# A gated state-space block with its backward pass on one core: half-array products side by side, kernel sums in one run, wide parameter products, single weight transposes, stores from GpSimd

## The chip, the cores and the metric

The kernel runs on one core of a Trainium2 chip. The core has a matrix engine (PE, with its weight loads listed as PEld), a vector engine (DVE), a scalar engine (ACT), a general engine (POOL, also called GpSimd), a sync engine (SP) that here only issues DMAs, and 16 DMA engines. SBUF is the on-chip memory, PSUM the memory that matrix products are added up in[...]. The metric is the device time of one execution in microseconds (us); the median of several runs is compared.

## What is computed

The reference is a block of one sequence of L = 2048 tokens and D = 576 channels, and its gradients for a given output gradient. Everything is bf16 in memory.

```python
xn = layernorm(x)                                   # x: 2048 x 576
K[d,l] = Re sum_n C[d,n] * exp(dt[d]*A[d,n]*l) * dt[d]*B[d,n]      # n = 128 states
s  = causal_convolution(xn, K) + xn * Dskip         # reference: by FFT along the tokens
h  = silu(xn @ w1) * (xn @ w3)                      # w1, w3: 576 x 4608
g  = silu(h @ w2)                                   # w2: 4608 x 576
out = x + s * g
# returned: out and the gradients of x, A, B, C (real and imaginary), log_dt, Dskip, w1, w3, w2
```

## The kernel before

All of it is one program of some 42,000 instructions, written with tile pools: a tile is a buffer of a pool, and a new tile of the same name waits until an earlier one of that name is free. The instructions of each engine run in one fixed order. That order is made when the program is built, by a list scheduler: `at(us)` (line 83) gives what follows a due time, and instructions that could go next are taken by due time. The due times are a planner's numbers and not times of the chip; changing one moves instructions in an engine's order.

The work, by its place in the trace of before:

- **0 to 133 us, prologue.** Layer norm, the transposed activations xnT, selectors and exponentials for the convolution kernel, spectra of the input.
- **133 to 531, forward products and kernel sums.** `ffn_hidden` (L688) makes the gate and up products: for each of 9 blocks of 512 hidden columns and each of 16 token tiles, one PSUM tile `pgu` of two banks. D = 576 is four full slices of 128 rows and a rest of 64. The full slices are L719. The two rests, of w1 and of w3, lie in the lower and the upper half of the partitions of one weight tile `wtail`, and their products (L720, L721) use half of the array's rows each. ACT and DVE evict `pgu` (L722, L724, L725); SP stores h and POOL stores gate and up (`gu_t` to `GI_dram`, L728). Between them `ssm_kernel` (L418) makes the convolution kernel in 36 chunks of 16 channels: `kgen_chunk` (L455) makes the factors q (stored to `Q_dram`), pz (three planes: minus P, Z, P; POOL makes the first as the negative of the third at L477; stored to `PZ_dram`), and v; `kgen_sum` (L490) multiplies q by v in 64 small products into `kps` (L500), each of 64 output rows by 16 columns. Each channel of a sum has its own due time, spread over the chunk's share.
- **531 to 830, forward tail.** `forward_tail` (L731): h by w2 (nine weight tiles `w2g`, loaded by POOL at L769), silu, the spectral convolution, and the transposes of the gradient `go_o` into `goT` (L833, four of 128 columns and one of 64 for each tile of tokens).
- **about 800 to 1593, hidden gradients.** `backward` (L1079) takes 18 groups of 256 hidden columns. `phase6_load` loads gate and up into tiles of the ring X and Y (L1193, L1194, POOL) and w2 rows (`w2r`, POOL, L1152) which SP transposes into `w2T`; `phase6_group` (L1211) multiplies `goT` by `w2T` into `ph` (L1226), ACT casts it to `gh` (L1229), DVE multiplies it into the two hidden gradients (L1232), and the weight gradients follow (L1273 and the functions `phase6_grad2`, `phase6_grad13`). The hidden gradients are stored by SP to `GU_dram` and `GG_dram` at the group's end (L1239). Until about 1300 `conv_bwd_quarter` (L886) makes the backward convolution beside this, with sums over the partitions by a column of ones (L917), and stores its spectra to `gK_dram`.
- **from 1300, parameter chunks.** `param_chunk` (L970), 36 of them, 19 beside the last groups and 17 beside the input gradient. Each loads the spectra gz, a transposed q (`qT`) and pz, makes two half chunks of products in two PSUM tiles `et_ps` each (L989), multiplies them by the planes of pz with DVE (L996, two sums s times two parts r) and reduces them into `S_all` (L998). Five `final_block`s (L1010) turn `S_all` into the gradients of A, B, C and dt; their due times stand in `final_at`.
- **1593 to 2000, input gradient.** `phase6_inputs` (L1288): for 16 tiles of tokens the two hidden gradients are read transposed (`ggc`, `guc`) and multiplied by the transposed w1 and w3 (L1333). These weights are made by DMA transposes from DRAM in `wT_into` (L1131), one for each of the five slices of D, into `wTA` (12 of 36 blocks, early), `wTB` (12), the memory of goT (4) and of go_o (8).

All DMA transposes are issued by SP through `nat_transpose` (L1140).

## Time and profile before

| | us |
|---|---|
| median of five runs | 2008.13 |
| the five runs | 2001.21, 2006.64, 2008.13, 2019.79, 2030.61 |
| the profiled execution | 2002.15 |
| its span, first to last instruction | 2000.4 |
| busy: PE, DVE, ACT, POOL | 1764.7, 1419.9, 1024.6, 269.5 |
| PE: gate and up products (L719) | 283.8 |
| PE: the two 64-row tails (L720, L721), in the stretch 133 to 531 | 55.9 each, side by side |
| PE: kernel sums (L500), in the same stretch | 57.1 |
| DVE: parameter products (L996) and reduces (L998) | 186.7 and 175.7 |
| POOL: negation of a factor (L477) | 55.5 |

The mean granted clock of PE in this execution was 0.965 of full speed. A row of instruction groups names line, engine, operation, output and inputs, shapes and count, then the busy time in us and the mean duration in ns of one, then the idle time of the engine just before them and what ended it. A row of a timeline begins with start and duration in us, and ends, in brackets, with the idle time before it and its releaser. An engine name with q (SPq) means that the row is the issuing of a DMA. Matmuls are pipelined: a duration of 0.39 us can stand for a start every 0.216.

### The profile page before, as it was taken

The page shows a single profiled execution, that of the slowest core. Times are in us where ns is not written, and L with a number is a line of the kernel's source. Part 1 is how long each engine was busy: PE and PEld are TensorE (multiplying, and loading weights), DVE is VectorE, ACT ScalarE, POOL GpSimd, SP SyncE. Part 2 cuts the span into 40 slices and gives each one's busy share as a digit, 9 for nine tenths or more (in the row PEclk, how much of TensorE's full clock was granted, in tenths as well). Part 3 has the DMA queues.
Part 4 walks back from the last instruction along what each step waited for, and adds up shares of the span by engine and source line. Part 5 has one row for each costly group of instructions (what it writes and reads, how often), then busy time and mean ns, then how long its engine had stood idle before and what let it go on. Part 6 is the DMA issues. An engine that isn't in the chain of part 4 may idle for free. (4 is left out here: it accounts for less than half of the span.)

```text
span 2000.4 us, 41956 instructions
## 1 busy us (share of the span) xinstructions
PE 1764.7 (88%) x17179; PEld 1292.0 (65%) x17179; DVE 1419.9 (71%) x2660; ACT 1024.6 (51%) x1739; POOL 269.5 (13%) x362
## 2 busy tenths in 40 slices
PE   2789999999889988989889898969999967989788
PEld 1544444444478866877778777758787845767666
DVE  7538888888477753486983859748989913489686
ACT  2778888888545555765666646526445200100112
POOL 4003333333322221000000000100000000000000
PEclk9899999999899999999999999989999978999999
DMA  3579888787966687365563654798998999999992
GB/s 86 190 284 320 308 292 297 275 313 277 301 188 157 164 216 230 114 185 165 172 185 112 184 160 151 191 246 226 237 233 219 208 197 187 198 197 218 211 187 58
DMA packets 612906, 417.10 MB, mean 209 GB/s; under 512 B 400394, under 2 KB 558058, under 8 KB 607978
## 3 DMA queue, kind: packets, MB, share of 16 engines
q1 hardware_dynamic: 547200, 280.47, 56.6%
q0 software_dynamic: 24288, 106.94, 15.5%
q10 hardware_dynamic: 41226, 27.02, 5.0%
q8 instruction: 134, 2.20, 0.5%
q14 instruction: 58, 0.48, 0.1%
HBM read 134.06 MB, written 188.01 MB: 161 GB/s over the span
## 5 line engine op out<-in xcount | busy, mean ns | idle before, releaser
L719 PE MATMUL pgu<-wmB_w,xnT 128*128 128x512 bf16 x1152 | 283.8, 382 | 1.2 <-ACT E_k L392 1.2
L1273 PEld LDWEIGHTS <-xn_bf 128*128 128x128 bf16 x2304 | 223.9, 98 | 29.3 <-issue 2.5
L1273 PE MATMUL pgw<-Y,xn_bf 128*128 128x256 bf16 x2048 | 232.1, 273 | 1.7 <-ACT gw L1275 1.6
L996 DVE TENSOR_TENSOR pr_q<-et_ps,pz 128x512 f32<-128x512 f32 x288 | 186.7, 686 | 42.5 <-PE et_ps L989 37.2
L1226 PE MATMUL ph<-w2T,goT 128*128 128x256 bf16 x1440 | 190.1, 280 | 22.8 <-ACT gh L1229 22.7
L719 PEld LDWEIGHTS <-xnT 128*128 128x128 bf16 x1152 | 103.5, 98 | 124.9 <-issue 20.4
L998 DVE TENSOR_REDUCE S_all<-pr_q 128x16 f32<-128x1024 f32 x144 | 175.7, 1220 | 2.2
L1226 PEld LDWEIGHTS <-goT 128*128 128x128 bf16 x1440 | 140.2, 100 | 33.4 <-issue 13.7
L1232 DVE TENSOR_TENSOR Y<-gh,Y 128x1024 bf16<-128x1024 bf16 x128 | 87.1, 689 | 101.2 <-ACT gh L1229 99.4
L1275 ACT CAST gw<-pgw 128x256 bf16<-128x256 f32 x144 | 54.0, 376 | 199.2 <-PE pgw L1273 197.4
L785 PE MATMUL po<-w2g,hc 128*128 128x288 bf16 x1152 | 152.3, 290 | 4.0 <-DMA hc<-H_dram 4.0
L1333 PEld LDWEIGHTS <-ggc 128*128 128x128 bf16 x1152 | 113.7, 100 | 51.9 <-DMA wTB<-in_B_w_dram 10.9
L1333 PEld LDWEIGHTS <-guc 128*128 128x128 bf16 x1152 | 114.0, 100 | 44.8 <-DMA guc<-GU_dram 13.6
L785 PEld LDWEIGHTS <-hc 128*128 128x128 bf16 x1152 | 112.2, 99 | 32.9 <-DMA hc<-H_dram 4.3
L1373 ACT ACTIVATE X<-X 128x576 f32<-128x576 f32 x16 | 10.9, 684 | 220.8 <-DVE X L1343 220.8
L1254 PE MATMUL pgw<-go_o,X 128*128 128x288 bf16 x896 | 120.7, 289 | 0.0
L722 ACT ACTIVATE s_t<-pgu 128x512 bf16<-128x512 f32 x144 | 87.4, 609 | 53.5 <-PE pgu L721 53.2
L1229 ACT CAST gh<-ph 128x512 bf16<-128x512 f32 x144 | 84.1, 617 | 52.5 <-PE ph L1226 33.4
L1254 PEld LDWEIGHTS <-X 128*128 128x128 bf16 x960 | 93.8, 99 | 23.9 <-issue 0.2
L582 PEld LDWEIGHTS <-dSi 128*128 128x128 bf16 x768 | 76.2, 100 | 35.3 <-issue 34.3
L467 DVE TENSOR_SCALAR m_k<-et_ps 128x512 int32<-128x512 int32 x108 | 74.1, 686 | 34.2 <-DMA E_l<-E_dram 18.2
L728 POOL DMA_DIRECT2D GI_dram<-gu_t x72 | 68.5, 952 | 205.7 <-DVE gu_t L724 169.5
(328 smaller groups left out, 3993.3 us busy)
## 6 DMA issues: line engine op xcount, KB each, us to landing
GI_dram<-gu_t POOLq DMA_DIRECT2D x72, 512.0 KB, 5.7
Y<-GI_dram POOLq DMA_DIRECT2D x19, 1024.0 KB, 6.1
H_dram<-h_t SPq DMA_DIRECT2D x72, 256.0 KB, 5.3
Q_dram<-q_k SPq DMA_DIRECT2D x36, 512.0 KB, 5.1
X<-GI_dram POOLq DMA_DIRECT2D x18, 1024.0 KB, 7.9
GU_dram<-Y SPq DMA_DIRECT2D x34, 512.0 KB, 5.2
GG_dram<-Y SPq DMA_DIRECT2D x30, 512.0 KB, 5.2
E_dram<-E_k SPq DMA_DIRECT2D x18, 768.0 KB, 3.7
```

Of the source, the lines that this page charges most:

```text
L582: nc.tensor.matmul(pv, lhsT=mat[:, kt, sl], rhs=V[:, :, ri, kt, :], start=(i == 0), stop=(i == n - 1))
L719: nc.tensor.matmul(pgu[:, j], lhsT=xnT[:, c, ts], rhs=wm[w][:, c, :], start=(c == 0), stop=False)
L722: nc.scalar.activation(out=s_t[:, :, q, :], in_=pgu[:, 0].rearrange("p (g f) -> p g f", g=ng), func=ACT.Silu)
L785: nc.tensor.matmul(pos[k][:, pi_, 0:pw], lhsT=hcs[k][:, fi, :], rhs=w2[fi][:, po:po + pw], start=(fi == 0), stop=(fi == FT - 1))
L996: nc.vector.tensor_tensor(out=pr[:, r], in0=T[r][:], in1=pz[:, s + r, h * 8:h * 8 + 8, :][:, :, None, :] .to_broadcast([P, 8, 2, AV]), op= ...
L998: nc.vector.tensor_reduce(out=S_all[:, 2 * s:2 * s + 2, d0:d0 + 8].rearrange("p k d -> p d k"), in_=pr[:].rearrange("p r d k a -> p d k r ...
L1226: nc.tensor.matmul(ph[j][:, k, :].rearrange("p (a f) -> p a f", f=P), lhsT=lw, rhs=rh, start=(n == 0), stop=(n == nfull))
L1229: nc.scalar.copy(out=gh[:, j], in_=ph[j])
L1232: nc.vector.tensor_tensor(out=t_[:, sl], in0=gh.rearrange("p j t f -> p (j t) f"), in1=t_[:, sl], op=ALU.mult)
L1254: nc.tensor.matmul(pgw[pi_][:, 0:pw], lhsT=hn[:, tt, fl * P:(fl + 1) * P], rhs=go_o[:, tt, po:po + pw], start=(tt == 0), stop=(tt == LT - 1))
L1273: nc.tensor.matmul(pw_[:, 0:FG], lhsT=self.xn_bf[:, tt, c * P:(c + 1) * P], rhs=nat[:, tt, :], start=(tt == 0), stop=(tt == LT - 1))
L1333: nc.tensor.matmul(px[pi_][:, 0:pw], lhsT=act[:, fi, :], rhs=wT[ai][fi][:, po:po + pw], start=(fi == 0 and ai == 0), stop=(fi == FT - 1 an ...
```

## The change

1. `ffn_hidden`: for the second token tile of each pair the two tails come first, so that the tails of two neighbouring tiles, four products, stand in a row.
2. `kgen_sum`: all 64 products of a chunk have one due time.
3. `kgen_chunk` keeps two planes of pz; `PZ_dram` has two. `param_chunk` loads them and makes the third with DVE.
4. `param_chunk`: the tiles et_ps are laid out part first; one product of DVE for each r covers both sums (1,024 columns where two of 512 stood), and one reduce per half chunk takes 2,048 columns. `pr_q` stays one buffer, of twice the size.
5. `final_block` takes its work space from that same buffer (pool g_r, tile pr_q, one buffer).
6. `wT_into` issues one transpose where it issued five; `load_w2T` loads and transposes the two blocks of a group in one each.
7. `phase6_group` stores hidden gradients from POOL, in the loop, after every second step.
8. Two of the nine `w2g` tiles have a pool of their own and a due time 60 us earlier.
9. The column of ones becomes a square of ones, so its sums come out on all 128 rows; the last transpose of a tile at L833 takes 128 columns (the last 128 of D) and its lower half is not used.
10. Due times: parameter chunks from T1 + 12 at steps of 13 (before: T1 at 13.5), wTA's transposes at T2 - 90 and T2 - 54 (before: spread from T2 - 160).

```diff
@@ -426,7 +426,7 @@
         PS = bass.MemoryType.PSUM
-        self.PZ_dram = self.dram.tile([P, NCH, 3, DC, AV], BF16, name="PZ_dram")
+        self.PZ_dram = self.dram.tile([P, NCH, 2, DC, AV], BF16, name="PZ_dram")
@@ -468,20 +468,19 @@
         q = qvp.tile([P, DC, 2, BV], BF16, name="q_k")
-        pz = sb.tile([P, 3, DC, AV], BF16, name="pz_k")
+        pz = sb.tile([P, 2, DC, AV], BF16, name="pz_k")
...
                in1=src[:, 0:QW].rearrange("p (d b) -> p d b", b=BV), op=ALU.mult)
-            tt(out=pz[:, 1 + k].rearrange("p d a -> p (d a)"), in0=E[:, QW:], in1=src[:, QW:], op=ALU.mult)
+            tt(out=pz[:, k].rearrange("p d a -> p (d a)"), in0=E[:, QW:], in1=src[:, QW:], op=ALU.mult)
         nc.sync.dma_start(out=self.Q_dram[ch], in_=q[:].rearrange("p d k b -> p (d k b)"))
-        nc.gpsimd.tensor_scalar(out=pz[:, 0], in0=pz[:, 2], scalar1=-1.0, scalar2=None, op0=ALU.mult)
...
                 tt(out=o.rearrange("p d (a x) -> p d a x", x=4),
-                   in0=pz[:, 1 + r].rearrange("p d (a x) -> p d a x", x=4),
+                   in0=pz[:, r].rearrange("p d (a x) -> p d a x", x=4),
@@ -492,8 +491,8 @@
         kps = ps1.tile([P, DC, AH], FP32, name="kps")
+        self.at(T)
         for dl in range(DC):
-            self.at(T + TK * dl / DC)
@@ -714,11 +713,13 @@
                     pgu = ps.tile([P, 2, FB], FP32, name="pgu")
-                    for j, w in enumerate(("B_w1", "B_w3")):
-                        for c in range(nfull):
-                            nc.tensor.matmul(pgu[:, j], lhsT=xnT[:, c, ts], rhs=wm[w][:, c, :], start=(c == 0), stop=False)
-                    nc.tensor.matmul(pgu[:, 0], lhsT=xnT[0:rem, nfull, ts], rhs=wt[0:rem, :], start=False, stop=True)
-                    nc.tensor.matmul(pgu[:, 1], lhsT=xnT[rem:P, nfull, ts], rhs=wt[rem:P, :], start=False, stop=True)
+                    steps = [(j, slice(0, P), c, wm[w][:, c, :]) for j, w in enumerate(("B_w1", "B_w3")) for c in range(nfull)]
+                    tails = [(0, slice(0, rem), nfull, wt[0:rem, :]), (1, slice(rem, P), nfull, wt[rem:P, :])]
+                    steps = tails + steps if q else steps + tails
+                    for n, (j, rows, c, w) in enumerate(steps):
+                        nc.tensor.matmul(pgu[:, j], lhsT=xnT[rows, c, ts], rhs=w,
+                                         start=all(st[0] != j for st in steps[:n]),
+                                         stop=all(st[0] != j for st in steps[n + 1:]))
@@ -751,6 +752,7 @@
         ep1 = rpool(fw, "o_ep1", 1)
+        wpoolE = rpool(fw, "o_wE", 1)
@@ -762,10 +764,10 @@
             nc.gpsimd.memset(t_[rem:P, nfull, :], 0.0)
-        w2g = [wpool.tile([P, GRP, D], BF16, name=f"w2g{n}") for n in range(FT // GRP)]
+        w2g = [(wpoolE if n < 2 else wpool).tile([P, GRP, D], BF16, name=f"w2g{n}") for n in range(FT // GRP)]
...
         for n, t_ in enumerate(w2g):
-            self.at(T0 - 4 + 2.5 * n)
+            self.at(T0 - 4 + 2.5 * n - (60 if n < 2 else 0))
@@ -816,9 +818,9 @@
             nc.gpsimd.memset(t_[rem:P, nfull, :], 0.0)
-        self.w2rows = [rowp.tile([P, DT * P], BF16, name=f"w2r{i}") for i in range(4)]
+        self.w2rows = [rowp.tile([P, self.FG // P, DT * P], BF16, name=f"w2r{i}") for i in range(2)]
         for w2r in self.w2rows:
-            nc.gpsimd.memset(w2r[:, D:DT * P], 0.0)
+            nc.gpsimd.memset(w2r[:, :, D:DT * P], 0.0)
@@ -829,12 +831,13 @@
             ptr = tps.tile([P, 1024], BF16, name="ptr")
-            for c, (do, dsz) in enumerate(cfg.dch):
-                nc.tensor.transpose(ptr[0:dsz, c * P:(c + 1) * P], go_o[:, i, do:do + dsz], self.ident_bf[:])
+            for c in range(nfull + 1):
+                do = min(c * P, D - P)
+                nc.tensor.transpose(ptr[:, c * P:(c + 1) * P], go_o[:, i, do:do + P], self.ident_bf[:])
...
                            in_=ptr[:, 0:nfull * P].rearrange("p (c t) -> p c t", t=P))
-            nc.vector.tensor_copy(out=self.goT[m][0:rem, nfull, ts], in_=ptr[0:rem, nfull * P:(nfull + 1) * P])
+            nc.vector.tensor_copy(out=self.goT[m][0:rem, nfull, ts], in_=ptr[P - rem:P, nfull * P:(nfull + 1) * P])
@@ -855,7 +858,7 @@
             nc.vector.tensor_scalar(out=self.lcol[:], in0=self.lcol[:], scalar1=1.0 / 512, scalar2=None, op0=ALU.mult)
-            self.ones_col = kp.tile([P, 1], BF16, name="ones_col")
+            self.ones_col = kp.tile([P, P], BF16, name="ones_col")
@@ -868,6 +871,7 @@
                 self.tc.tile_pool(name="g_r", bufs=1, side="right") as rp:
+            self.rp = rp
@@ -914,7 +918,7 @@
             for tt in range(KT):
-                nc.tensor.matmul(gds[0:1, 0:W], lhsT=self.ones_col[:], rhs=prod[:, tt, :], start=(b == 0 and tt == 0),
+                nc.tensor.matmul(gds[:, 0:W], lhsT=self.ones_col[:], rhs=prod[:, tt, :], start=(b == 0 and tt == 0),
@@ -980,23 +984,26 @@
             pz = qp.tile([P, 3, 16, AV], BF16, name="pz")
-            nc.sync.dma_start(out=pz[:], in_=self.PZ_dram[:, ch])
+            nc.sync.dma_start(out=pz[:, 1:3], in_=self.PZ_dram[:, ch])
+            nc.vector.tensor_scalar(out=pz[:, 0], in0=pz[:, 2], scalar1=-1.0, scalar2=None, op0=ALU.mult)
             for h in range(2):
-                T = [ps.tile([P, 8, 2, AV], FP32, name="et_ps") for _ in range(2)]
+                T = [ps.tile([P, 2, 8, AV], FP32, name="et_ps") for _ in range(2)]
...
                     for r in range(2):
-                        nc.tensor.matmul(T[r][:, dd].rearrange("p k (f t) -> p (k f) t", f=2), lhsT=qT[:, dl, :],
-                                         rhs=gK[:, r, :, :, dl, :].rearrange("p k f t -> p (k f) t"),
+                        nc.tensor.matmul(T[r][:, :, dd].rearrange("p k (f t) -> p k f t", f=2), lhsT=qT[:, dl, :],
+                                         rhs=gK[:, r, :, :, dl, :],
...
                 d0 = h * (D // 2) + ch * 8
-                for s in range(2):
-                    pr = rp.tile([P, 2, 8, 2, AV], FP32, name="pr_q")
-                    for r in range(2):
-                        nc.vector.tensor_tensor(out=pr[:, r], in0=T[r][:], in1=pz[:, s + r, h * 8:h * 8 + 8, :][:, :, None, :]
-                                                .to_broadcast([P, 8, 2, AV]), op=ALU.mult)
-                    nc.vector.tensor_reduce(out=S_all[:, 2 * s:2 * s + 2, d0:d0 + 8].rearrange("p k d -> p d k"),
-                                            in_=pr[:].rearrange("p r d k a -> p d k r a"), op=ALU.add, axis=AX.XY)
+                pr = rp.tile([P, 2, 4, 8, AV], FP32, name="pr_q")
+                for r in range(2):
+                    nc.vector.tensor_tensor(out=pr[:, r].rearrange("p (s k) d a -> p s k (d a)", s=2),
+                                            in0=T[r][:].rearrange("p k d a -> p k (d a)")[:, None]
+                                            .to_broadcast([P, 2, 2, 8 * AV]),
+                                            in1=pz[:, r:r + 2, h * 8:h * 8 + 8, :].rearrange("p s d a -> p s (d a)")
+                                            [:, :, None, :].to_broadcast([P, 2, 2, 8 * AV]), op=ALU.mult)
+                nc.vector.tensor_reduce(out=S_all[:, :, d0:d0 + 8], in_=pr[:].rearrange("p r k d a -> p k d r a"),
+                                        op=ALU.add, axis=AX.XY)
@@ -1026,7 +1033,8 @@
         S2 = ST[v].rearrange("p (r s) n -> p s r n", s=2)[:, 1]
-        A, B = [fp.tile([P, 4, N], FP32, name=f"f{n}")[v] for n in range(2)]
+        ws = self.rp.tile([P, 2, 4, 8, cfg.AV], FP32, name="pr_q")[v].rearrange("p r k d a -> p (r k d a)")
+        A, B = [ws[:, n * 4 * N:(n + 1) * 4 * N].rearrange("p (k n) -> p k n", n=N) for n in range(2)]
@@ -1104,10 +1112,10 @@
                 t = wA.tile([P, FA, D], BF16, name=f"wTA{ai}")
-                self.wT_into(t[:], ai, 0, wT, lambda c: T2 - 160 + 12 * (2 * c + ai))
+                self.wT_into(t[:], ai, 0, wT, T2 - 90 + 36 * ai)
...
             N1 = 19
-            chunk_at = lambda ch: T1 + 13.5 * ch if ch < N1 else T2 + TX * 1.4 + 13.5 * (ch - N1)
+            chunk_at = lambda ch: T1 + 12 + 13 * ch if ch < N1 else T2 + TX * 1.4 + 13.5 * (ch - N1)
@@ -1130,9 +1138,8 @@
         n = dst.shape[1]
-        for c, (do, dsz) in enumerate(self.cfg.dch):
-            self.at(at(c))
-            self.nat_transpose(dst[:, :, do:do + dsz], self.aps[("B_w1", "B_w3")[ai]][do:do + dsz, f0 * P:(f0 + n) * P])
+        self.at(at)
+        self.nat_transpose(dst, self.aps[("B_w1", "B_w3")[ai]][:, f0 * P:(f0 + n) * P])
@@ -1146,11 +1153,10 @@
         w2T = self.wp.tile([P, nfl, cfg.DT, P], BF16, name="w2T")
-        for fl in range(nfl):
-            fi = gi * nfl + fl
-            w2r = self.w2rows[fi % len(self.w2rows)]
-            nc.gpsimd.dma_start(out=w2r[:, 0:cfg.D], in_=self.aps["B_w2"][fi * P:(fi + 1) * P, :])
-            self.nat_transpose(w2T[:, fl], w2r[:])
+        w2r = self.w2rows[gi % len(self.w2rows)]
+        nc.gpsimd.dma_start(out=w2r[:, :, 0:cfg.D], in_=self.aps["B_w2"][gi * self.FG:(gi + 1) * self.FG, :].rearrange(
+            "(l p) d -> p l d", p=P))
+        self.nat_transpose(w2T[:].rearrange("p l c f -> p (l c) f"), w2r[:].rearrange("p l d -> p (l d)"))
@@ -1231,12 +1237,13 @@
                                         op=ALU.mult)
+            if s % 2 == 1:
+                ts = slice(s // 2 * LH, (s // 2 + 1) * LH)
+                for (dst, t_) in ((self.GU_dram, gu), (self.GG_dram, gg)):
+                    nc.gpsimd.dma_start(out=dst[ts, :, gi * FG:(gi + 1) * FG].rearrange("t p f -> p t f"),
+                                        in_=t_[:, ts, :])
...
                 self.phase6_grad2(gi, s // 2, hn, ps_gw, "pgw")
-        for (dst, t_) in ((self.GU_dram, gu), (self.GG_dram, gg)):
-            for j in range(2):
-                ts = slice(j * LH, (j + 1) * LH)
-                nc.sync.dma_start(out=dst[ts, :, gi * FG:(gi + 1) * FG].rearrange("t p f -> p t f"), in_=t_[:, ts, :])
@@ -1305,7 +1312,7 @@
                 for ai in range(2):
-                    self.wT_into(tiles[ai], ai, f0, wT, lambda c: t)
+                    self.wT_into(tiles[ai], ai, f0, wT, t)
```

## The prediction

> **What bounds the kernel now.** I read the busy shares and slices first, then a table of busy time by stage, and then the timelines of the stages that the change touches.
>
> ```profile
> PE 1764.7 (88%) x17179; PEld 1292.0 (65%) x17179; DVE 1419.9 (71%) x2660; ACT 1024.6 (51%) x1739; POOL 269.5 (13%) x362
> PE   2789999999889988989889898969999967989788
> DMA  3579888787966687365563654798998999999992
> ...
> 133.00:531.00 398.00, 393.62 (x3853) 172.28 (x3852) 323.56 (x595) 320.84 (x378) 131.67 (x122) 1.00 0.85 293
> 830.00:1300.00 470.00, 424.59 (x4332) 363.24 (x4330) 351.81 (x726) 288.84 (x663) 25.82 (x44) 0.97 0.55 160
> 1300.00:1593.00 293.00, 266.36 (x2852) 226.24 (x2850) 248.25 (x340) 129.22 (x215) 10.92 (x21) 0.97 0.93 227
> 1593.00:1700.00 107.00, 75.81 (x595) 57.27 (x594) 24.04 (x37) 6.87 (x17) 0.00 (x0) 0.84 1.05 197
> ```
>
> In each row of the stage table the stretch is followed by its length and the busy us of PE, PEld, DVE, ACT and POOL. From 133 to 531 (forward products and kernel sums) PE is busy 393.6 of 398 us: only work of PE itself counts there. Later, PE leaves 45 us of 470, 27 of 293 and 31 of 107; the DMA engines are full from 1300 on. So two questions: which PE time is not multiplication, and what ends PE's waits in the last 700 us.
>
> PE in the first stretch, start and duration of each run of matmuls:
>
> ```profile
> 300.81 0.81 PE L719 MATMUL pgu<-wmB_w,xnT 128*128 128x512 bf16 x3
> 301.55 0.39 PE L720 MATMUL pgu<-wtail,xnT 64*128 64x512 bf16 x1
> 301.55 0.39 PE L721 MATMUL pgu<-wtail,xnT 64*128 64x512 bf16 x1
> 301.87 1.47 PE L719 MATMUL pgu<-wmB_w,xnT 128*128 128x512 bf16 x6
> 303.40 0.55 PE L500 MATMUL kps<-v_k,q_k 128*64 128x16 bf16 x24
> ```
>
> Full 512-column products start 0.216 us apart. The two 64-row tails already start together, but the last full product starts 0.31 us before them, and the next one 0.32 us after: about 0.10 us is lost on entering and 0.10 on leaving. Kernel sums (64 output columns) cost the same at both ends; over the trace the gaps are 0.31 to 0.32 where 0.216 is the product, and 0.227 against 0.123 ahead of the one-column sums at L917. I call it 0.10 us a switch.
>
> The later waits, one line each from PE's, ACT's, SP's and DVE's timelines:
>
> ```profile
> 539.86 0.64 PE L626 MATMUL et_ps<-KT,dSf 128*128 128x144 bf16 x4 [9.21 <-ACT gu_t L724]
> 1305.80 1.44 PE L989 MATMUL et_ps<-gz,qT 128*128 128x64 bf16 x24 [5.47 <-DMA gz<-gK_dram]
> 1345.11 1.07 ACT L1229 CAST gh<-ph 128x512 bf16<-128x512 f32 x2 [12.74 <-DMA wTA<-in_B_w_dram]
> 1610.79 21.59 SPq L1140 DMA_TRANSPOSE wTB<-in_B_w_dram  x10
> 1633.88 0.66 PE L1333 MATMUL px<-wTB,ggc 128*128 128x288 bf16 x2 [10.82 <-DMA wTB<-in_B_w_dram]
> 1897.11 0.42 DVE L1034 TENSOR_TENSOR f<-rates 128x256 f32<-128x256 bf16 x1 [15.66 <-ACT gout L1050]
> ```
>
> They show a 9.2 us stall after the forward products; a 5.5 us one at the first parameter chunk, whose spectra gz have just been written; ACT held 12.7 us while SP issues weight transposes (PE then waits 10.8 us for its cast); SP itself taking 21.6 us for ten transposes while PE waits; and DVE waiting 15.7 us for a final block's outputs.
>
> **What the Trainium skill says.** "TensorEngine Tiling (Array Packing)", Key Properties: "Changing tiling mode (not just tile) drains the TensorE". The trace agrees, at 0.10 us a change. "VectorE: DVE Perf Modes", the TRN2 errata: a float32 two-operand product takes (N+151)/0.96 ns; for N = 512 that is 691, the trace has 686 (L996), and its reduce of 1,024 has 1,220 where the formula gives 1,224. "DMA: Bandwidth & Descriptors", Issuing engines are not separate DMA queues: moving a transfer to another engine saves only that engine's issuing time. The trace doesn't test this; I price the moved stores so.
>
> **Part by part**, against the profiled run of 2002.15 us (span 2000.40 and 1.75 outside). It lies 6.0 us below the median.
>
> *Side-by-side tails and sums in one run.* Only the place of the tails and the due time of the sums change; the number of products stays. In the built order of PE's instructions I counted changes of shape class (64 rows, 64 columns, full) in this stage: 464 before, 296 after. The tails stand in 66 runs of four and 14 fragments instead of 144 pairs, the sums in 68 runs instead of 119. 168 x 0.10 = 16.8 us. PE has nothing to hide it behind, and DVE and ACT (324 and 321 of 398 us) have room to follow. Against it: a sum run waits for its v and q in one piece. I take -16, ends -18 and -8.
>
> *One-column sums* (L917) get 128 columns: 46 changes gone, 4.5 us. The weight load grows from 1 to 128 columns and lies beside matmuls. *Transposes* at L833 become full: 32 changes gone, about 2 us (149 and 176 ns around them against 62 to 110). DVE at 352 of 470 covers some of it: -6 together, ends -7 and -2.
>
> *w2 loads.* Nine loads on POOL stand near 518 to 537, ahead of stores whose completion frees gu_t for ACT: the 9.2 us stall. Two of them now issue at about 130, before the first GI store, behind waits on early PE and ACT work; the GI stores, and with them gu_t, are queued behind. They carry 1.2 MB, about 4 us at that stretch's 293 GB/s. The other seven still stand among the last GI stores. -4, ends -8 and +2.
>
> *Negated factor.* POOL's 36 x 1.54 = 55.5 us (L477) go, off the path; each factor store and load is 256 KB instead of 384, 4.6 us to landing before. DVE gets 36 negations of 128x512 bf16 in the backward, unseen before; the plain products of that size take 0.42, I take 0.3 (0.2 to 0.45).
>
> *Wide parameter products.* Per half chunk, two pairs at 1.30 and two reduces at 1.23, in all 5.06 (from the chain), become two 1,024-wide products and one 2,048-wide reduce. Formula: 1.22 and 2.29 as single durations, less 0.04 of overlap each: 4.6. So 10.1 becomes 9.2 + 0.3 = 9.5 per chunk, over 36 chunks 22 us of DVE (bounds 0 and 30: the wider forms aren't in the trace). The two PSUM banks come free after one product each instead of two. Where DVE ends PE's wait (28 us of L989 waits after 1593) some of this is on the path; I take -5, ends -15 and +3.
>
> *Chunk times.* The built order puts about 24 us of PE work ahead of the first chunk's products: the gz stall has time to go, -4, ends -5.5 and 0.
>
> *Merged transposes.* Each ten-part weight transpose becomes two of up to 6,912 packets of 256 B; every packet remains. SP needed 21.6 us for wTB's 13,824 packets (640 per us), but 12.24 for 9,216 in the second tile's ggc and guc (753). At that rate 18.4, so 3 us; go_o 14.3 to 12.2, 2 us. PE's waits there stand behind the same queue. But ACT's own DMA issues are held while SP issues, and one piece is now some 9 us long. For 1593 on: -3, ends -10 and +8. For wTA near 1335, now placed just ahead of the first chunk: the 10.8 us stall becomes up to two of some 5: -2, ends -11 and +8.
>
> *w2T pairs* (36 to 18 transposes and loads): SP loses 18 issues of about 1.2 us floor, off the path, zero. It costs a few us per group if the two-block load comes late.
>
> *Stores on POOL.* 72 GU and GG stores, 1,024 rows of 512 B each, leave SP for POOL. POOL has 952 ns for GI_dram stores of 512 KB and 1,024 rows; I take 1.0 to 1.4, 72 to 101 us on an engine busy 25.8 of 470. In its queue they stand ahead of the next Y, X and w2r loads, and each waits for DVE's product at L1232; SP loses those waits, so its transposes come earlier. Loads took 6 us to land, groups are about 40 us apart. +2, ends -6 and +15.
>
> *Final blocks.* Their workspace is now pr_q, a single buffer, so the next chunk's product waits for ACT's reads. In DVE's new order tile work follows block 0, which removes one stall (6 us); after blocks 3 and 1 the next product follows directly and stays behind ACT. -2, ends -8 and +10.
>
> Sum: -16 - 6 - 4 - 5 - 4 - 3 - 2 + 2 - 2 = -40. 2002 becomes 1962; with the 6 us offset, a median of 1968.
>
> **Rivals.** (a) *Only the switches pay*, and the backward keeps its waits because full DMA engines set them: -16 - 6 + 2, about 1988. For it: DMA share 1.05 in 1593 to 1700, packets unchanged. Against: much of PE's idle there is order, not volume. (b) *All stalls go*: -16 - 6 - 8 - 12 - 5 - 10 - 5 - 6, near 1940. The stores and the single buffer speak against it. (c) *Slower: loads behind stores on POOL.* If a group's Y or X load comes behind a store that waits for the previous group's DVE product, all 18 groups start late. It decides when the slip exceeds the slack of a load; POOL sat 15 to 20 us before those loads until their buffer came free, so the buffer, not the queue, is now last. From 3.5 us per group on: 18 x 3.5 = 63, less 40, gives about 2031. (d) *The runs don't form as ordered or a run of tails still drains between its pairs*: without the 16 us, about 1984. Against it, both orders are fixed at build time, and consecutive kernel sums start 16.5 ns apart without a drain.
>
> **Chances.** Forecast 0.58, (a) 0.18, (b) 0.12, (c) 0.08, (d) 0.04. Range 1940 to 2008: it reaches over (a), and cuts off most of (c) and the far half of (b). A measurement of this kernel tells about 1% (20 us) from no change. Faster by over that: the forecast but for its upper end, (b), and half of (a) and (d): 0.77; within it 0.14; slower 0.09.
>
> **What would show it.** Up to 531: PE's tails in fours, 0.10 us once per run, and the end of the last pgu product 14 to 18 us earlier. No 9.2 us stall after it, or half of it. No gz stall. pr_q groups at 1.2 and S_all at 2.3 us. ACT's idle before gh near wTA under 8 us. GU and GG stores on POOL at 1.0 to 1.4 us, and loads not released by them. PE's idle from 1593 to 1700 below 31 us. The forecast fails if ACT or PE waits 10 us for a merged transpose more than once, if Y and X loads land after the first product that reads them, or if DVE's pr_q waits on ACT's gout after most final blocks.

## The result, and the profile after

The changed kernel takes 2030.55 us (median of 37 runs, 2007.85 to 2061.23), the kernel before in the same comparison 2013.49 (72 runs). The ratio is 1.0078, 95% interval 1.0059 to 1.0097: slower by 0.8%, where 1968 us, 2% faster, was forecast and the range ended at 2008. The profiled execution took 2023.6 us, span 2021.8.

Busy shares and slices of the changed kernel:

```profile
PE 1755.0 (87%) x17179; PEld 1293.1 (64%) x17179; DVE 1405.3 (70%) x2480; ACT 1027.1 (51%) x1739; POOL 271.9 (13%) x378
PE   2789999999799988989889898969899958979788
DMA  3588888887976697465563655898988799789883
```

The same stretches of its span as before (length, then busy PE, PEld, DVE, ACT, POOL, and last the granted clock, the DMA share and GB/s):

```profile
133.00:531.00 398.00, 381.04 (x3846) 167.18 (x3845) 317.68 (x593) 324.69 (x378) 72.73 (x84) 0.99 0.83 280
830.00:1300.00 470.00, 422.61 (x4421) 366.10 (x4419) 347.58 (x717) 287.24 (x670) 52.49 (x70) 0.99 0.54 161
1300.00:1593.00 293.00, 254.32 (x2666) 214.57 (x2664) 221.28 (x233) 131.27 (x215) 39.79 (x48) 0.95 0.90 209
```

PE is busy 10 us less in all (1755.0 for 1764.7), but has more idle time: 17 us of the first stretch, where it had 4, and 39 of the third, where it had 27. Its granted clock was also at half speed for longer: 163 us of the changed trace, leaving out the first 100, for 134 before. There a product of 288 columns starts every 0.240 us instead of 0.123. Summed over neighbouring products of one shape, I estimate that this costs PE 40 us for 33 before. Of the 163 us, 143 are in stretches that begin within 10 us of a PE idle time of 2 us or more, so a stall goes with slower products as well; that it causes them was not tested. To find the places I compared the two traces at equal work: the time at which PE has done the same sum of product time (0.213 us for 512 columns and in proportion, about 0.017 for a small kernel sum, a pair of tails once).

| work done, us | time before | time after | difference |
|---|---|---|---|
| 75 (forward products start) | 154.7 | 157.2 | +2.5 |
| 375 (near their end) | 506.5 | 507.5 | +1.0 |
| 400 | 546.1 | 552.8 | +6.7 |
| 550 | 715.0 | 719.2 | +4.2 |
| 625 (groups begin) | 812.2 | 824.0 | +11.8 |
| 1025 | 1280.4 | 1285.9 | +5.5 |
| 1050 (first chunk) | 1315.2 | 1313.6 | -1.6 |
| 1075 | 1352.6 | 1358.1 | +5.5 |
| 1150 | 1431.2 | 1446.5 | +15.4 |
| 1300 (groups end) | 1591.6 | 1613.9 | +22.3 |
| 1500 | 1853.0 | 1882.3 | +29.3 |
| 1600 | 1986.4 | 2007.8 | +21.3 |

So the 16 us of the forward products don't appear: the last of them ends at 535.6, for 530.7 before. Another 24 us are lost between 1050 and 1300 us of work, beside the parameter chunks. What DVE and PE wait for from 1290 on (waits: engine, tile, line, releaser; us in total, times, longest):

```profile
DVE pz L988 <- DMA pz<-PZ_dram: 118.3, 21, 28.4
PE et_ps L994 <- DVE pr_q L1000: 43.5, 30, 8.1
```

L988 is the new negation. DVE waits 118.3 us for its input. Before, it had no wait of this kind, and PE's wait for pr_q was

```profile
PE et_ps L989 <- DVE pr_q L996: 33.4, 29, 10.2
```

One of the 21, in DVE's timeline:

```profile
1422.53 0.69 DVE L1214 TENSOR_TENSOR Y<-Y,X 128x1024 bf16<-128x1024 bf16 x1
1431.68 0.29 DVE L988 TENSOR_SCALAR pz<-pz 128x512 bf16<-128x512 bf16 x1 [8.46 <-DMA pz<-PZ_dram]
1431.89 0.69 DVE L1215 TENSOR_TENSOR X<-Y,X 128x1024 bf16<-128x1024 bf16 x1
1432.49 1.22 DVE L1000 TENSOR_TENSOR pr_q<-et_ps,pz 128x1024 f32<-128x1024 f32 x1
```

and PE's and SP's at the same place:

```profile
1433.76 0.59 PE L994 MATMUL et_ps<-gz,qT 128*128 128x64 bf16 x8 [8.14 <-DVE pr_q L1000]
...
1409.67 9.05 SPq L1147 DMA_TRANSPOSE qT<-Q_dram  x1
1418.83 1.93 SPq L987 DMA_DIRECT2D pz<-PZ_dram  x1
```

The negation at 1431.68 is that of chunk 6. The pr_q right behind it is still a product of chunk 5: in the built order three of that chunk's four products come after chunk 6's negation. They need nothing of chunk 6, but DVE runs in order. The load of chunk 6 came late because SP runs in order too. Its buffer, one of two, was free from 1415.5, when the last product of chunk 4 ended, but SP was issuing a transpose until 1418.7, and the data landed at 1431.7. The wait for a transfer thus stands in front of the products whose end frees the PSUM tiles that PE waits for.

It is mostly SP's order, not the buffer. Of the 118.3 us, 32.7 fall on the first two chunks, which wait for no buffer; 81 on loads that SP issued 0.9 us or more after their buffer was free; only 4 on loads issued as soon as it was. The longest wait after the first, 20.1 us at 1683.5, is for a buffer free from 1655.0: SP issued the load at 1680.2, after a row of transposes for the input gradient and two gz loads.

Of 36 negations, 14 stand a whole chunk (four products) ahead of their own products.

### The profile page after: what moved, and what is told of

It is laid out like the page before. It is cut to its first block, busy times and chain, and to the rows that moved or that the text cites. A ratio compares the mean times of both kernels' runs of the same rounds, so it can differ in the third digit from the quotient of the medians.

```text
span 2021.8 us, 41553 instructions
## 1 busy us (share of the span) xinstructions
PE 1755.0 (87%) x17179; PEld 1293.1 (64%) x17179; DVE 1405.3 (70%) x2480; ACT 1027.1 (51%) x1739; POOL 271.9 (13%) x378
## 4 chain that ended last, share of the span: by engine, by line
PE 32%; DVE 26%; ACT 15%; DMA 15%; issue 5%; SPq 4%; POOL 0%; ACTq 0%; DVEq 0%; POOLq 0%
PE pgw L1280 6%; DMA pz<-PZ_dram 4%; DVE pr_q L1000 4%; PE px L1340 4%; PE pgw L1340 4%; SPq L1147 3%; PE pgu L720 3%; DVE S_all L1005 3%; PE po L787 3%; PE pgw L1261 2%; PE ph L1232 2%; ACT S_k L329 2%; ACT gk_st L950 2%; DVE cm_t L606 2%; DMA gs<-GS_dram 2%
## 5 line engine op out<-in xcount | busy, mean ns | idle before, releaser
L1280 PEld LDWEIGHTS <-xn_bf 128*128 128x128 bf16 x2304 | 225.7, 98 | 50.7 <-issue 22.3
L1280 PE MATMUL pgw<-Y,xn_bf 128*128 128x256 bf16 x2048 | 233.9, 274 | 19.5 <-ACT gw L1282 18.6
L720 PEld LDWEIGHTS <-xnT 128*128 128x128 bf16 (+1 forms) x1440 | 114.9, 97 | 191.5 <-issue 82.4
L1000 DVE TENSOR_TENSOR pr_q<-et_ps,pz 128x1024 f32<-128x1024 f32 x144 | 170.8, 1220 | 50.4 <-PE et_ps L994 38.4
L1232 PE MATMUL ph<-w2T,goT 128*128 128x256 bf16 x1440 | 187.9, 277 | 10.5 <-ACT gh L1235 10.3
L1005 DVE TENSOR_REDUCE S_all<-pr_q 128x32 f32<-128x2048 f32 x72 | 164.4, 2284 | 0.9
L787 PE MATMUL po<-w2g,hc 128*128 128x288 bf16 x1152 | 153.2, 291 | 10.9 <-DMA hc<-H_dram 6.6
L1340 PEld LDWEIGHTS <-ggc 128*128 128x128 bf16 x1152 | 114.7, 101 | 51.8 <-issue 12.4
L1380 ACT ACTIVATE X<-X 128x576 f32<-128x576 f32 x16 | 10.9, 684 | 238.6 <-DVE X L1350 238.0
```

Source lines behind the costliest of these rows:

```text
L720: nc.tensor.matmul(pgu[:, j], lhsT=xnT[rows, c, ts], rhs=w, start=all(st[0] != j for st in steps[:n]), stop=all(st[0] != j for st in steps ...
L787: nc.tensor.matmul(pos[k][:, pi_, 0:pw], lhsT=hcs[k][:, fi, :], rhs=w2[fi][:, po:po + pw], start=(fi == 0), stop=(fi == FT - 1))
L1000: nc.vector.tensor_tensor(out=pr[:, r].rearrange("p (s k) d a -> p s k (d a)", s=2), in0=T[r][:].rearrange("p k d a -> p k (d a)")[:, None ...
L1005: nc.vector.tensor_reduce(out=S_all[:, :, d0:d0 + 8], in_=pr[:].rearrange("p r k d a -> p k d r a"), op=ALU.add, axis=AX.XY)
L1232: nc.tensor.matmul(ph[j][:, k, :].rearrange("p (a f) -> p a f", f=P), lhsT=lw, rhs=rh, start=(n == 0), stop=(n == nfull))
L1280: nc.tensor.matmul(pw_[:, 0:FG], lhsT=self.xn_bf[:, tt, c * P:(c + 1) * P], rhs=nat[:, tt, :], start=(tt == 0), stop=(tt == LT - 1))
```

## Experiments

Ratios are to the kernel before, run on the same chip in the same round, with their 95% intervals; they need not be the quotient of the medians given here. The changed kernel's own is 1.0078 (1.0059 to 1.0097).

**The negation, taken out.** GpSimd makes it in the forward part again:

```diff
-        pz = sb.tile([P, 2, DC, AV], BF16, name="pz_k")
+        pz = sb.tile([P, 3, DC, AV], BF16, name="pz_k")
...
+        nc.gpsimd.tensor_scalar(out=pz[:, 0], in0=pz[:, 2], scalar1=-1.0, scalar2=None, op0=ALU.mult)
...
-            nc.vector.tensor_scalar(out=pz[:, 0], in0=pz[:, 2], scalar1=-1.0, scalar2=None, op0=ALU.mult)
```

> The changed kernel with the negated factor made by GpSimd in the forward part again: three planes stored and loaded, no negation on DVE. Theory: in the changed kernel DVE stands for 57.5 us (10 waits, from 1290 to 1620) at the negation, whose input a transfer still brings, and PE waits behind it; with the negation gone these waits go, and the stretch of the parameter chunks and the input gradient gets 12 to 25 us shorter: about 2008 to 2018 where the changed kernel has 2030. Rival (the merged transposes delay the transfers, and DVE would wait for the same factor one instruction later): less than 5 us gained, DVE's wait moves to the first product pr_q.

Measured 1997.2 us, ratio 0.9859 (0.9815 to 0.9903): 2.2% below the changed kernel's ratio, 33 us by the medians and more than expected. DVE's waits for pz from 1290 on are 27.6 us in three, 25.5 of them at the first chunk. The rival, that the wait only moves on to pr_q, falls. The profiled executions are 33 us apart as well. PE's waits for pr_q are 16.6 us less (26.9 for 43.5), its stall near 1335 is 6.2 less (11.1 for 17.3), and by the estimate above its products lose some 10 us less at half clock.

**The negation on DVE, but behind the products of the chunk before.** It writes a tile of its own in a pool with one buffer, which those products read:

```diff
+            pn = rp.tile([P, 16, AV], BF16, name="pn")
...
-            nc.vector.tensor_scalar(out=pz[:, 0], in0=pz[:, 2], scalar1=-1.0, scalar2=None, op0=ALU.mult)
+            nc.vector.tensor_scalar(out=pn[:], in0=pz[:, 1], scalar1=-1.0, scalar2=None, op0=ALU.mult)
```

> The changed kernel, negation still made by DVE from two stored planes, but into a tile of its own with a single buffer: it can't be queued until the products of the chunk before have read that buffer. In DVE's order it now stands at most two products ahead of its own, where in the changed kernel it often stands four ahead (a whole chunk). DVE makes one more instruction per half chunk (two products of 512 for one of 1,024), some 0.1 us each. Theory (the cost is the place of the negation: DVE waits there for a transfer that is issued only when the chunk before the last is done): nearly all is recovered, 1995 to 2008. Rival (the cost is DVE's own time or the two-plane transfers): it stays above 2022.

1996.2 us, 0.9889 (0.9822 to 0.9955), 1.9% below the changed kernel's ratio. The same 36 negations, the same two-plane transfers, more instructions on DVE, and the loss is gone. The 22.8 us that are left are at the first chunk:

```profile
DVE pn L989 <- DMA pz<-PZ_dram: 28.7, 3, 22.8
PE et_ps L995 <- DVE pr_q L1001: 18.9, 13, 8.1
```

In DVE's order 29 of the negations now stand directly ahead of their own products, and 7 one product earlier. So it is the place in DVE's queue that costs, not the operation.

**The negation alone**, put into the kernel before (item 3 of the change, all else untouched):

```diff
-            nc.sync.dma_start(out=pz[:], in_=self.PZ_dram[:, ch])
+            nc.sync.dma_start(out=pz[:, 1:3], in_=self.PZ_dram[:, ch])
+            nc.vector.tensor_scalar(out=pz[:, 0], in0=pz[:, 2], scalar1=-1.0, scalar2=None, op0=ALU.mult)
```

> The kernel before with this one edit: two planes, the negation on DVE in the parameter chunks. In DVE's order it stands six of a chunk's eight products ahead of its own in most chunks. Theory: the same waits of DVE on pz, 40 us or more in all, slower than before by 15 to 35 us (ratio 1.007 to 1.018). Rival (only together with the merged transposes or the stores on GpSimd is the load late): within 8 us of before.

2060.1 us, 1.0237 (1.0165 to 1.0310): about 48 us slower, more than expected. It needs neither the merged transposes nor the stores on GpSimd:

```profile
DVE pz L983 <- DMA pz<-PZ_dram: 133.6, 24, 31.7
```

**The wide products alone**, with the shared work space of the final blocks (items 4 and 5 of the change on the kernel before):

```diff
-                for s in range(2):
-                    pr = rp.tile([P, 2, 8, 2, AV], FP32, name="pr_q")
...
+                pr = rp.tile([P, 2, 4, 8, AV], FP32, name="pr_q")
```

> The kernel before with the wide products and reduces alone, and the final blocks' work space in the same buffer, since there is no memory for both. From the changed kernel's durations (1.18 a product and 2.29 a reduce) a half chunk takes 4.65 where it took 5.06; theory: DVE saves 0.8 us a chunk, 30 us, of which a third is on the path: -4 to -14 us. Rival: the shared buffer's waits for ACT eat it, within 4 us of before.

1991.5 us, 0.9892 (0.9860 to 0.9923): 22 us, more than both theories. The instructions cost what was expected (groups of the changed kernel):

```profile
L1000 DVE TENSOR_TENSOR pr_q<-et_ps,pz 128x1024 f32<-128x1024 f32 x144 | 170.8, 1220 | 50.4 <-PE et_ps L994 38.4 <-ACT gout L1058 10.3
L1005 DVE TENSOR_REDUCE S_all<-pr_q 128x32 f32<-128x2048 f32 x72 | 164.4, 2284 | 0.9
```

The shared buffer is a small burden: 10.3 us of DVE's waits on ACT's gout in all there, 21 in a_neg_own; before, DVE waited 31.3 for gout.

**The forward products.** First the sums' due times put back in the changed kernel, then each part alone on the kernel before:

```diff
-        self.at(T)
         for dl in range(DC):
+            self.at(T + TK * dl / DC)
```

> The changed kernel with the kernel sums of a chunk spread over due times as before. In the built order PE has 99 more changes of shape, 10 us at 0.10 each. Theory: the run of 64 sums is what brings the selector products of the chunk generator too close together (single buffer, freed by DVE), which costs 12 us of new waits; these go back from 20.9 to about 9 us, so the stretch of the forward products stays as long within 3 us. Rival: the waits come from the tails or from DVE, and stay; then the stretch grows by 10 us and the whole is about 2040.

2028.7 us, 1.0113 (1.0073 to 1.0153): no gain. By the starts of PE's products between 134 and 507, changes of shape cost 43.9 us before, 27.7 in the changed kernel, 37.1 here; all other waits 8.9, 20.9 and 13.8. The run of sums saves 9 us of changes and brings 7 us of waits, of the 12 that the theory had. PE's waits for DVE's m_k, which frees the selector's buffer, are 1.0 us before, 10.9 in the changed kernel and 0.7 here; other small waits take part of their place. One of them (changed kernel, PE):

```profile
163.04 1.24 PE L720 MATMUL pgu<-wmB_w,xnT 128*128 128x512 bf16 x5
165.35 0.38 PE L466 MATMUL et_ps<-SEL,lhs_t 128*128 128x512 bf16 x1 [1.07 <-DVE m_k L467]
165.57 0.81 PE L720 MATMUL pgu<-wmB_w,xnT 128*128 128x512 bf16 x3
166.31 0.61 PE L720 MATMUL pgu<-wtail,xnT 64*128 64x512 bf16 x4
```

The tails stand in fours as planned. The selector product at 165.35 waits for DVE to free its single buffer.

> The kernel before with side-by-side tails, the square of ones and full transposes, and nothing else. In the built order PE has 444 changes of shape where before has 591: 14.7 us at 0.10 each. Theory: these come through, since nothing else in the order of the selector products changes: -10 to -15 us, the last forward product 5 to 8 us earlier. Rival (PE's gain is taken back by waits on DVE and DMAs as in the changed kernel): within 5 us of before.

Items 1 and 9 of the change on the kernel before: 2011.5 us, 0.9975 (0.9940 to 1.0011), about 5 us where 10 to 15 were expected, and not clear of no change. Its last forward product ends no earlier than before (531.2 for 530.7), and the stall behind it is 18.6 us for 9.2.

> The kernel before with the kernel sums of a chunk due in one piece, and nothing else: 541 changes of shape for 591, 5 us less. Theory: selector products come closer together and PE waits more for DVE to free their one buffer: 5 to 10 us of new waits, so 0 to +5 us in all. Rival: the new waits in the changed kernel came from the tails, and this is 4 to 6 us faster.

Item 2 alone on the kernel before: 2023.1 us, 1.0084 (1.0058 to 1.0109). This is 17 us slower, over both theories, and by itself as large as the whole change's loss. The place is not among the products but just behind them. One or two lines each of POOL, ACT and PE, in b_sums:

```profile
513.14 3.75 POOL L769 DMA_DIRECT2D w2g<-in_B_w_dram  x5
519.69 0.91 POOL L728 DMA_DIRECT2D GI_dram<-gu_t  x1 [2.80 <-DVE gu_t L724]
...
550.30 1.01 ACT L724 CAST gu_t<-pgu 128x1024 bf16<-128x1024 f32 x1 [21.34 <-DMA GI_dram<-gu_t]
...
552.77 0.64 PE L626 MATMUL et_ps<-KT,dSf 128*128 128x144 bf16 x4 [22.34 <-ACT gu_t L724]
```

The GI store of 519.69 is issued behind five w2 loads and lands only at 550.3, 30.6 us later; ACT waits for the buffer that it frees, and PE for ACT. Before, the store in the same place, issued at 522.28, landed after 15.1 us. It is the 9.2 us stall of before, grown to 22.3, which is 13 of the 17 us. The next GI store (541.19) stood on POOL for 17.7 us, until the first of these loads had landed. In the runs it goes with the median time that the nine w2 loads take to land:

| run | w2g to landing, us | PE's stall, us |
|---|---|---|
| before | 13.1 | 9.2 |
| best1 | 14.1 | 11.5 |
| b_shapes | 21.4 | 18.6 |
| np_sp | 24.9 | 17.6 |
| a_neg_pool | 25.4 | 19.8 |
| b_sums | 30.4 | 22.3 |

(In the changed kernel, with two of the loads early, landing takes 14.5 and the stall is in pieces of 1.7, 4.8, 4.3 and 1.5 us.)

To take the two apart I used kernels whose DMA transposes are plain loads of the same bytes (so that the first `hc`, which SP transposes beside the w2 loads, is a plain load too), with the loads on POOL or on SP:

```diff
-        self.nc.sync.dma_start_transpose(out=dst, in_=src)
...
+            self.nc.sync.dma_start(out=dst, in_=src.rearrange("a (n b) -> a n b", n=n))
...
-            nc.gpsimd.dma_start(out=t_[:], in_=aps["B_w2"][n * GRP * P:(n + 1) * GRP * P, :].rearrange(
+            nc.sync.dma_start(out=t_[:], in_=aps["B_w2"][n * GRP * P:(n + 1) * GRP * P, :].rearrange(
```

A w2 load from SP in a kernel that keeps its transposes was not run.

> The kernel before with every DMA transpose replaced by a plain load of the same bytes, so that the weights and activations read in that way are not transposed and what is made from them is another result. The order of GpSimd's instructions is unchanged and no transpose runs before the last forward products, so the trace can be read up to about 550 us. Control: PE's stall after the forward products is 8 to 11 us, as the 9.2 of before.

> The same with the kernel sums in one piece (b_sums). As in b_sums the stall is 18 to 24 us, behind ACT, a GI store and seven w2 loads in GpSimd's queue.

> The same with the kernel sums in one piece, and the nine w2 loads issued by SP instead of GpSimd. Theory: GpSimd's queue with the loads ahead of the GI stores is what makes the saving a stall; GpSimd now waits under 4 us ahead of each of the last GI stores, and PE's stall is under 8 us. Rival (the transfers are slow on any queue, or ACT waits for something else): the stall stays over 15 us.

> The same with the kernel sums as before and the nine w2 loads issued by SP. Theory: the stall falls to 2 to 6 us from 9. Rival: no change, since the h stores stand behind the loads on SP then.

The stalls were 6.5 us (pl_b), 4.0 (pl_b_sums), 1.6 (pl_b_sums_w2sp) and 1.6 (pl_b_w2sp); their whole times, 1910.8 to 1919.5, say nothing of this change. Two expectations missed: the control has 6.5 us for 8 to 11, and without the transpose the run of sums makes no long stall, with w2g landing after 12.7 us. So the third had little left to show, and the fourth came out just below its 2 to 6. In these kernels the loads ahead of the stores on POOL carry what stall there is: without them in that queue it falls from 6.5 and 4.0 to 1.6. The long delay comes only with the transpose. The stretch 512 to 532 of before, b_sums and pl_b_sums, in that order (the last two columns are the DMA share and GB/s):

```profile
512.00:532.00 20.00, 18.41 (x143) 7.37 (x142) 8.08 (x13) 8.64 (x13) 9.71 (x13) 1.00 1.06 307
```

```profile
512.00:532.00 20.00, 18.43 (x79) 6.52 (x78) 5.71 (x6) 7.12 (x11) 7.09 (x9) 0.92 1.20 124
```

```profile
512.00:532.00 20.00, 19.61 (x139) 7.51 (x135) 7.07 (x9) 8.25 (x13) 9.06 (x12) 0.91 1.02 355
```

With the transpose in b_sums the engines are just as busy and move a third. Why the same overlap costs before so much less, where SP issues that transpose 5 us later (516.9 for 511.9) and in 5.1 us instead of 11.7, is not settled.

**The other parts.** Weight transposes in five parts again, in the changed kernel:

```diff
-        self.at(at)
-        self.nat_transpose(dst, self.aps[("B_w1", "B_w3")[ai]][:, f0 * P:(f0 + n) * P])
+        for c, (do, dsz) in enumerate(self.cfg.dch):
+            self.at(at(c))
+            self.nat_transpose(dst[:, :, do:do + dsz], self.aps[("B_w1", "B_w3")[ai]][do:do + dsz, f0 * P:(f0 + n) * P])
```

> The changed kernel with each weight transpose in five parts again, wTA's at their earlier due times. Theory: the two wTA transposes of 7.5 and 10.3 us ahead of the first chunk delay gz, qT and pz and hold ACT's own DMA issue for 20 us, and PE loses 17.3 us there; in parts this becomes a stall of some 10 us as before or less, -5 to -12 us at 1340; after 1593 PE's first wait is 2 to 6 us longer than with the merged ones. Total -2 to -8 against the changed kernel. Rival: the hold comes from the chunk's place in the queue and not from the size of the transposes: no gain at 1340, +3 to +6 in all.

2037.6 us, 1.0130 (1.0098 to 1.0163): no gain, and by the ratios some 10 us slower than the changed kernel, with intervals that just miss each other. The chain at wTA gets better, as expected (at 1100 us of work about 2.5 us ahead of before, where the changed kernel is about 6.5 behind), and the input gradient gives it all back: from its first to its last product 387 us, for 374 in the changed kernel and 380 before.

> All three of these undone together in the changed kernel. If the three act separately, their differences add up; theory: 2005 to 2015, about the kernel before or somewhat under it, because side-by-side tails, the square of ones and the wide products remain. Rival: they act on the same waits and the sum falls short, or another part (stores on GpSimd, the shared work space) keeps it above 2020.

The edits of a_neg_pool, a_sums_spread and a_wT_split together: 2004.8 us, 0.9856 (0.9788 to 0.9924), no better than taking out the negation alone.

The next two go on from a_neg_pool. First item 8 undone:

```diff
-            self.at(T0 - 4 + 2.5 * n - (60 if n < 2 else 0))
+            self.at(T0 - 4 + 2.5 * n)
```

> The changed kernel with the negation on GpSimd in the forward part, as in the run a_neg_pool, and the nine w2 loads due together as before. Theory: the early loads did not help (PE stood 4.8 and 4.3 us in two places after the forward products where it stood 9.2 in one): within 4 us of a_neg_pool's 1997. Rival: the early loads shorten this place, and without them it is 5 to 8 us slower.

2007.8 us, 0.9925 (0.9883 to 0.9967). It decides nothing: with three planes the memory of the two early loads is free only at the end of the forward part, and in a_neg_pool they stand at 514 as well. The two kernels differ little, and their intervals overlap.

Then item 7 undone, from GpSimd to SP:

```diff
-                    nc.gpsimd.dma_start(out=dst[ts, :, gi * FG:(gi + 1) * FG].rearrange("t p f -> p t f"),
+                nc.sync.dma_start(out=dst[ts, :, gi * FG:(gi + 1) * FG].rearrange("t p f -> p t f"), in_=t_[:, ts, :])
```

> The changed kernel with the negation on GpSimd in the forward part (a_neg_pool), and the hidden gradients stored from SP at the group's end again. Theory: the stores on GpSimd were free, since DMA time is the same and no load waited behind them: within 5 us of a_neg_pool's 1997. Rival 1: they made SP's transposes come earlier; on SP it is 6 to 12 us slower. Rival 2: they held the loads of groups; on SP it is 5 us or more faster.

1983.5 us, 0.9861 (0.9815 to 0.9907), the same ratio as a_neg_pool. No cost or gain of the storing engine is seen; with these intervals one of some 10 us could hide.

Last, the edits of b_wide and b_shapes together on the kernel before:

> The kernel before with the wide products (and the shared work space) and with side-by-side tails, square of ones and full transposes; no negation on DVE, no merged transposes, no run of sums, no early w2 loads, stores from SP. Theory: the two gains are in different stretches and add up: 20 or more us from the wide products (the run b_wide) and 10 to 15 from the shapes, 30 to 38 us below the kernel before, ratio 0.981 to 0.985, ahead of every kernel so far. Rival: both remove the same waits later on: no better than b_wide alone, 0.989.

1982.5 us, 0.9869 (0.9820 to 0.9917). It is ahead of both kernels, but not shown to be ahead of b_wide: the stall after the forward products is 11.5 us in it, for 8.5 in b_wide.

The four parts run alone on the kernel before (b_neg, b_wide, b_shapes, b_sums) add up to some 38 us slower, where the whole change is 16 slower. So they don't simply add, or the parts not run alone on that kernel gain; this was not separated.

## Why the prediction was wrong

- **The step that failed is the negated factor.** The prediction priced it as an instruction, 0.3 us, and that is right: 292 ns. It put at nothing the wait that the instruction brings, for a load that comes late in SP's order, and what is queued behind it: up to a chunk of products. That is 118.3 us of DVE's waits and 1.9 to 2.2% of the kernel (a_neg_own, a_neg_pool), where the prediction had some 10 us of busy time inside a gain. None of the rivals held it; Rival (c) looked for this kind of wait on POOL, where it was not. That the measured time lies so near the kernel before is no sign of small effects: large ones of both signs cancel in it.
- **Tails and sums.** 168 changes at 0.10 us, 16.8, was right on PE: 43.9 became 27.7. But the last forward product, forecast 14 to 18 us earlier, came 4.9 later. That DVE and ACT "have room to follow" was the error: 12 us came back as waits, most of them on the selector's single buffer (10.9 us), and the start was 2.5 us late. Room on average says nothing of a buffer that turns over once per product.
- **w2 loads.** Forecast -4. From 375 to 450 us of work the changed kernel loses 3.5. The prediction named the stall and its cause, but took its length as fixed.
- **Square of ones, full transposes.** Forecast -6; from 625 to 1025 us of work 6.3 us are gained, which agrees; no run isolates it.
- **Wide products.** Sizes right (1.22 and 2.28); value mis-sized: -5 and -2 for the shared buffer, measured -22 together (b_wide). It is the largest gain of the change, hidden by the negation.
- **Chunk times.** The gz stall of 5.5 us is gone, and 7 us are gained at the first chunk. Right in kind, and more than the range's end of 5.5.
- **Merged transposes.** Near wTA the prediction had two stalls of 5 for one of 10.8; it was one of 17.3, with ACT held 19.9 us. PE and ACT:

```profile
1340.77 5.79 PE L1280 MATMUL pgw<-Y,xn_bf 128*128 128x256 bf16 x32 [17.28 <-ACT gw L1282]
...
1340.35 0.65 ACT L1282 CAST gw<-pgw 128x256 bf16<-128x256 f32 x2 [19.94 <-DMA pz<-PZ_dram]
```

  The prediction's reason, that ACT's own DMA issues are held while SP issues, is not what the trace shows. ACT stands at a semaphore in front of its store of gw (L1283). That semaphore reports the landing of SP's pz load of the first chunk (issued at 1323.8, landed at 1339.8), the load that DVE waits for as well. In both traces the transfers of SP and ACT take turns on eight semaphores; before, ACT's store at 1344.54 waited in this way for a wTA transpose that landed at 1344.52. After 1593 PE's wait for wTB fell from 10.8 to 3.2 and 4.3, and its wait for ACT's gw rose from 7.5 to 12.4. Summed as -5; a_wT_split suggests more, but it also moves wTA's due times.
- **Stores on POOL.** 0.9 us each, 64 us in all, just under the forecast 1.0 to 1.4; no cost seen (np_sp). Rival (c) falls: 63 us would have shown.
- **Final blocks.** One stall of 9.2 us for ACT's gout is left of three (6.0, 15.7 and 8.9). Within the bounds.

Open: 7.6 us lost between 550 and 625 us of work, where PE waits for goT (9.2 for 5.4) and hc (6.6 for 4.0).

The Trainium skill says in "DMA: Bandwidth & Descriptors", Issuing engines are not separate DMA queues, that another issuing engine saves only the time of issuing; np_sp agrees within its interval (0.9861 and 0.9859). The drain on a change of tiling mode that it states in "TensorEngine Tiling (Array Packing)", Key Properties, agrees with the 16.2 us of changes saved. The formula that the prediction took from "VectorE: DVE Perf Modes", the TRN2 errata, is stated there for a float32 addition; that it fits products and reduces is what the traces here show (1.220 us for 1.224, and 2.284 for 2.291).

## What to carry to other kernels

An instruction moved to another engine takes its input's wait along: ask when that input can land, what stands ahead of its load in the order of the engine that issues it, and what stands behind the instruction in its new engine's order. If a scheduler decides the order, tie the instruction to what it must not overtake, by a buffer that the earlier work still reads. And before counting on time saved in a stage bound by one engine, look at the first wait behind the stage.

## What was not expected of the hardware

Plain loads beside a DMA transpose: w2g of 576 KB landed after 30.4 us in b_sums, 12.7 where that transpose was a plain load, with the DMA engines full both times, at 124 and 355 GB/s. A transpose alone is not enough: the kernel before has it too, with 13.1 us and 307 GB/s.
